# Four engines read the attention test's sum itself, TensorE alone reads the copy, and the copy sits in the fourth-last row's buffer

## The chip, the cores and the metric

The kernel runs on one core of a Trainium2 chip: TensorE (PE), VectorE (DVE), ScalarE (ACT), GpSimd (POOL) and SyncE (SP), with 16 DMA engines. The metric is the device time of one execution in microseconds; lower is better.

## The reference

A window attention with four sink keys feeds a gated MLP block. Cut to what is computed:

```python
scores = q @ k.T / sqrt(64)                    # 4 batches, 8 heads, 768 x 768
keep   = (col < 4) | (0 <= row - col < 128)    # 4 sink keys and a window of 128
a      = softmax(where(keep, scores, -1e9))
x      = heads_side_by_side(a @ v)             # (4, 768, 512)
h      = gelu_tanh(x @ w_in)                   # (4, 768, 1024)
u, v   = halves(h)
v_n    = (v - mean(v)) / sqrt(var(v) + 1e-6) * g_ln
v_s    = w_sg @ v_n + b_sg                     # over the 768 positions
out    = x + (u * v_s) @ w_out                 # float32
```

## The kernel before, in words

**Two programs in one.** The main program takes the exponentials without subtracting the row maximum. That is good as long as every row sum and its reciprocal stay in range. A second, general program (`general`, from L1250) subtracts the maximum; it stands behind `tc.If(found["total"] < COUNT)` at L1306 and is skipped when the test says that the main program was good. The test is small: on GpSimd two comparisons of all reciprocals with bounds (`compare`), a product with ones on TensorE (`tally`), a sum on VectorE (`summed`), which leaves one integer, `total`. All of it is done in the last fifth of the kernel, ahead of the last batch's output rows.

**The branch.** Every engine has its own instruction stream and decides for itself, so each of the five has to load the integer into a register (`ask`, L1126, a TENSOR_LOAD in the trace) and then branches (L1306). SP loads `total` in the op `peek` and ACT in `peek_act`, both in the middle of the last batch. PE, DVE and POOL load it in the last op, `look`. They don't load `total` but a copy of it. The op `copied` (L1140) writes the copy on VectorE into column 0 of an output row's buffer, `held_o`. That buffer is the one of output row block `MARK`, and since it is being stored to HBM, the copy waits for that store to have landed. In this way the three engines reach the branch only when the copy is made.

**After the branch.** An engine that skips the general program adds to its own semaphore what the general program would have added. POOL does so too for the eight semaphores of its own DMA queue (waits on them, then one INC_SWDGE_SEM). Behind that come the instructions that end the program, which the trace puts at L1338: SP waits for the semaphores of all queues and engines, two in one wait, and then all engines meet in two rounds, with a clearing of the semaphores by POOL between them.

**Order.** Nothing is scheduled at run time: `FIRST` lists the names of all ops in the order in which they are emitted, and each engine runs its own in that order. `Planner.run` walks that list; a `Buf` is counted open in its room until its last user was emitted. The list ends in the last batch's output rows: `pj3t` (product on PE), `o3t` (residual added on DVE, L918) and `store3t` (SP, L928) for t = 2, 1, 0, 3, 4, 5, then row block 3 of batch 2, kept for last and cut in halves: `pj23x o23x store23x` with its store on SP, and `pj23y o23y store23y` with its store on ACT. Behind these stand `copied` and `look`. So block (3, 4), the `MARK` of the kernel before, is the third-last row block and block (3, 3) the fourth-last.

Of the kernel before, what the change touches and what calls it, by code (L numbers as in the profile page):

```python
# [9 lines left out]
I32 = mybir.dt.int32  # L10
# [39 lines left out]
class Planner:  # L50
# [15 lines left out]
    def add(self, *args, **kwargs):  # L66
        op = Op(*args, **kwargs)
        self.ops.append(op)
        return op
# [86 lines left out]
    "look"  # L156
)
TAKERS = (
    "zero_a0:ACT zero_a1:DVE zero_a2:DVE zero_a3:DVE low_a:DVE zero_b0:DVE zero_b1:DVE "
# [19 lines left out]
def kernel(  # L179
# [16 lines left out]
    B, H, S, Dh = q.shape  # L196
# [45 lines left out]
    add = plan.add  # L242
# [10 lines left out]
    WARM = 8  # L253
    AHEAD = (0, 1)
    LAST = (2, 3)
    MARK = (B - 1, 4)
    LONG = ()
    BY_DMA = (11,12,13,14,15)
    W_DMA = ()
# [21 lines left out]
    total = consts.tile([128, 1], I32, name="total")  # L281
# [53 lines left out]
    def make_mask(m, at):  # L335
        for h in range(2):
# [6 lines left out]
                    rank=-2000)  # L343
    T["dark0"] = add("dark0", {"DVE": 450}, lambda _: make_dark0(), [T["dark"]], use=[dark],
                     rank=-1998)
# [5 lines left out]
    if LONG:  # L351
        T["spread"] = add("spread", {"POOL": 900}, lambda _: make_spread(), new=[spread],
                          rank=-378)
# [658 lines left out]
    def turn_g(_):  # L1012
# [4 lines left out]
    a = add("turn_g", {"PE": 330}, turn_g, [T["g_row"], T["one"]], new=[g_ps], use=[g_row],  # L1017
            rank=9000)
# [39 lines left out]
    for n in range(NP):  # L1058
        r = 100 * n
# [26 lines left out]
    COUNT = 2 * 128 * NP * NT * 2  # L1086
    flat = rcps.rearrange("p n c i h o -> p (n c i h o)")

    def compare(_):
# [8 lines left out]
    a = add("compare", {"POOL": 900}, compare,  # L1098
            [T["rcp", n, c] for n in range(NP) for c in range(2)],
            new=[fits], rank=12000)  # L1100
# [8 lines left out]
    a = add("tally", {"PE": 180}, tally, [a], new=[ps], use=[fits], rank=12900)  # L1109
# [6 lines left out]
    a = add("summed", {"DVE": 500}, summed, [a], use=[ps], rank=12900)  # L1116
    found = {}
# [2 lines left out]
              mybir.EngineType.SP]  # L1120

    WHY = "a sum of so many zeros and ones"
    ASKED = [mybir.EngineType.SP, mybir.EngineType.Activation]

    def ask(tile, engines):
        return nc.values_load(tile[0:1, 0:1], engines=engines, min_val=0, max_val=COUNT,  # L1126
                              skip_runtime_bounds_check_because=WHY)

    def peek(_):
        found["SP"] = ask(total, ASKED[0:1])

    def peek_act(_):
        found["ACT"] = ask(total, ASKED[1:2])

    held_o = T["o_sb", *MARK]

# [2 lines left out]

    def look(_):
        tc.mark_branch_hint_location("rest", HINT, engines=HINTED)
        rest = ask(held_o.tile[:, 0:1].bitcast(I32), [e for e in mybir.ALL_ENGINES if e not in ASKED])
        found["total"] = type(rest).of_register_unchecked(
            type(rest.val)([*found["SP"].val, *found["ACT"].val, *rest.val]), min_val=0,
            max_val=COUNT)

    for part in segments:
        for lead, follow in zip(part[0::2], part[1::2]):  # L1150
# [2 lines left out]
            follow.rank = plan.first.get(follow.name, -10000)  # L1153
    for t in range(NT):
        T["pj", B - 1, t].behind.append(a)
    add("peek", {"SP": 750}, peek, [a], rank=0)
    add("peek_act", {"ACT": 750}, peek_act, [a], rank=0)
    T["st", -1, 0] = add("copied", {"DVE": 150}, copied, [a, T["st", *MARK]], use=[held_o],
                         rank=0)
    add("look", {"SP": 1200}, look, [a, T["st", -1, 0]] + [T["st", B - 1, t] for t in range(NT)], rank=0)  # L1160
    plan.run()

# [180 lines left out]
```

## Time and profile before

| | |
|---|---|
| Runs | 162.61, 162.88 and 165.15 us; median 162.88 us |
| The profiled execution | 162.92 us, of which the span of the trace is 160.9 us |
| Busy share of the span | PE 94%, DVE 82%, ACT 67%, POOL 52% |
| Granted TensorE clock | 0.998 |
| Instructions | 4016 |

The span goes from the first to the last instruction of the trace; some 2.0 us of the execution lie around it. A busy share is an average over the whole kernel; the change touches what happens behind the last output rows, so the stretch that counts is the last few microseconds.

### The profile page before, as it was taken

Reading aid. Unit: us, or ns where it says so; the run is one execution under the profiler, and the core shown is the slowest. Engines: PE = TensorE matmul, PEld = TensorE weight load, DVE = VectorE, ACT = ScalarE, POOL = GpSimd, SP = SyncE. Lnnn points to the kernel's source line nnn. Section 1 sums busy time; section 2 is a strip of 40 time slices with the busy share of each in tenths; the row PEclk is TensorE's granted clock in tenths of the full one; section 3 lists DMA queues with packets and bytes.
Section 4 is the critical chain, followed back from the end, with each engine's and each line's share of the span. In section 5 each row is a group of like instructions: output and inputs, shape, how many; then the busy total and the mean of one; then the engine's idle time right before and its main releaser. Section 6 shows DMA issues by size and latency. Waiting matters only on the chain.

```text
span 160.9 us, 4016 instructions
## 1 busy us (share of the span) xinstructions
PE 151.2 (94%) x1562; PEld 87.7 (55%) x1562; DVE 132.3 (82%) x283; ACT 107.6 (67%) x143; POOL 83.5 (52%) x126
## 2 busy tenths in 40 slices
PE   6899999999999999999799999998999999999960
PEld 2454574667657576456555664545556545555530
DVE  7556887798897999789999989589999969888960
ACT  6198787897979797979686875747995187701100
POOL 3645944155899695287957743573779403200000
PEclk9999999999999999999999999999999999999999
DMA  4999999998999956999876879799966330130182
GB/s 152 332 247 311 194 169 201 203 304 265 344 306 295 275 143 182 328 238 259 141 218 154 194 188 257 131 297 256 215 172 175 114 130 0 65 134 0 65 322 82
DMA packets 67877, 32.42 MB, mean 201 GB/s; under 512 B 56564, under 2 KB 64772, under 8 KB 67856
## 3 DMA queue, kind: packets, MB, share of 16 engines
q1 hardware_dynamic: 65328, 29.26, 70.1%
q0 software_dynamic: 2384, 2.75, 10.6%
q8 instruction: 13, 0.21, 0.6%
q10 hardware_dynamic: 144, 0.13, 0.2%
q14 instruction: 8, 0.07, 0.1%
HBM read 24.81 MB, written 6.29 MB: 193 GB/s over the span
## 4 chain that ended last, share of the span: by engine, by line
PE 79%; DVE 8%; POOL 4%; DMA 4%; ACT 1%; issue 1%; SPq 0%; DVEq 0%; POOLq 0%; ACTq 0%
PE vs L864 20%; PE hv L751 11%; PE o_ps L907 11%; PE hu L793 10%; PE sc L610 9%; PE av L676 8%; PE cps L550 4%; PE sc L590 3%; DMA q_f<-in_q_dram 2%; DVE vn L840 2%; PE xps L726 2%; POOL mv L820 2%; DVE o_sb L918 2%; DMA out_dram<-o_sb 2%; DVE mv L826 1%; DVE ex L638 1%
## 5 line engine op out<-in xcount | busy, mean ns | idle before, releaser
L627 ACT ACTIVATE ex<-sc 128x1024 bf16<-128x1024 f32 x48 | 47.4, 1024 | 9.7 <-PE sc L610 9.6
L864 PE MATMUL vs<-wsgT,vn 128*128 128x384 bf16 x192 | 35.5, 326 | 1.4 <-DVE vn L840 1.1
L864 PEld LDWEIGHTS <-vn 128*128 128x128 bf16 x192 | 17.5, 98 | 13.1 <-DVE vn L840 1.5
L793 PE MATMUL hu<-xT,w_in_sb 128*128 128x384 bf16 x128 | 23.6, 326 | 0.8 <-DVE o_sb L918 0.8
L801 ACT ACTIVATE uT<-hu 128x384 bf16<-128x384 f32 x32 | 14.9, 489 | 12.3 <-PE hu L793 12.1
L907 PE MATMUL o_ps<-w_out_sb,gT 128*128 128x512 bf16 (+1 forms) x100 | 23.1, 371 | 0.0
L751 PE MATMUL hv<-w_in_sb,xT 128*128 128x512 bf16 x96 | 22.5, 379 | 0.0
L875 DVE SCALAR_TENSOR_TENSOR vs<-vs,g_sb,b_bc 128x384 f32<-128x384 f32 x32 | 19.6, 621 | 2.8 <-PE vs L864 1.2
L773 DVE BATCH_NORM_STATS2 st<-v_all 128x6 f32<-128x512 f32 x24 | 16.3, 677 | 6.3 <-ACT v_all L762 6.3
L249 POOL CAST cast<-k_f 128x768 bf16<-128x768 f32 x16 | 13.7, 858 | 14.1 <-DMA k_f<-in_k_dram 12.8
L610 PE MATMUL sc<-qT,kT 64*128 64x256 bf16 (+2 forms) x320 | 18.9, 249 | 0.4 <-ACT qT L247 0.4
L311 POOL TENSOR_SCALAR_AFFINE_SELECT ex<-ex 128x512 bf16<-128x512 bf16 (+1 forms) x23 | 15.1, 655 | 7.9 <-ACT ex L627 7.7
L676 PEld LDWEIGHTS <-ex 128*128 128x128 bf16 x480 | 16.7, 97 | 4.1 <-issue 1.4
L695 DVE TENSOR_TENSOR x<-av,rcps 128x384 bf16<-128x384 f32 x32 | 17.5, 552 | 0.9
L883 DVE TENSOR_TENSOR gT<-vs,uT 128x384 bf16<-128x384 f32 x32 | 17.5, 556 | 0.9
L676 PE MATMUL av<-v_sb,ex 128*128 128x65 bf16 x352 | 18.0, 194 | 0.1
L249 POOL CAST cast<-q_f 128x768 bf16<-128x768 f32 x15 | 13.1, 872 | 9.7 <-issue 4.6
L793 PEld LDWEIGHTS <-w_in_sb 128*128 128x128 bf16 x128 | 12.3, 98 | 9.7 <-issue 1.2
L918 DVE TENSOR_TENSOR o_sb<-o_ps,x 128x512 f32<-128x512 f32 (+1 forms) x25 | 16.2, 663 | 1.3 <-PE o_ps L907 1.2
L762 ACT ACTIVATE v_all<-hv 128x512 f32<-128x512 f32 x24 | 13.7, 598 | 5.2 <-PE hv L751 5.0
L249 POOL CAST v_sb<-v_f 128x768 bf16<-128x768 f32 x16 | 13.9, 869 | 2.3 <-DMA v_f<-in_v_dram 2.3
L751 PEld LDWEIGHTS <-xT 128*128 128x128 bf16 x96 | 9.2, 98 | 10.5 <-DVE xT L249 0.6
(71 smaller groups left out, 197.6 us busy)
## 6 DMA issues: line engine op xcount, KB each, us to landing
k_f<-in_k_dram SPq DMA_DIRECT2D x16, 384.0 KB, 5.9
q_f<-in_q_dram SPq DMA_DIRECT2D x16, 384.0 KB, 5.1
v_f<-in_v_dram SPq DMA_DIRECT2D x16, 384.0 KB, 5.9
out_dram<-o_sb SPq DMA_DIRECT2D x23, 256.0 KB, 2.2
wsg<-in_moe_w_sg_dram POOLq DMA_DIRECT2D x2, 576.0 KB, 10.5
w_in_sb<-in_moe_w_in_dram POOLq DMA_DIRECT2D x2, 512.0 KB, 7.6
w_out_sb<-in_moe_w_out_dram POOLq DMA_DIRECT2D x1, 512.0 KB, 7.8
b_bc<-in_moe_b_sg_dram SPq DMA_DIRECT2D x1, 384.0 KB
```

Of the source, the lines that this page charges most:

```text
L249: eng[e].tensor_copy(dst, src)
L610: nc.tensor.matmul(sc.tile[row:row + keys, h, col:col + m], kT.tile[rows, k0:k0 + keys], qT.tile[rows, q0:q0 + m], start=not by_pe, stop=n ...
L627: nc.scalar.activation(out=ex.tile, in_=sc.tile, func=AF.Exp, scale=scale)
L676: nc.tensor.matmul(av.tile[:, m, h, :], ex.tile[:, h, col:col + 128], val, start=first, stop=(m == HT - 1 and h == 1 and at == len(steps) ...
L695: nc.vector.tensor_mul(x.tile[:, hp, HT * c:HT * (c + 1), :].rearrange("p i (h d) -> p i h d", h=2), av.tile[:, :, :, 0:64], rcp.to_broadc ...
L751: nc.tensor.matmul(ps.tile[:, 0:512], xT.tile[:, c, 128 * j:128 * (j + 1)], w_in_sb[:, c, DF:], start=(c == 0), stop=(c == KD - 1))
L793: nc.tensor.matmul(ps.tile[:, 0:NH], w_in_sb[:, c, 128 * f:128 * (f + 1)], xT.tile[:, c, NH * m:NH * (m + 1)], start=(c == 0), stop=(c == ...
L864: nc.tensor.matmul(ps.tile[:, 0:NH], vn.tile[:, si, 128 * f:128 * (f + 1)], wsgT[:, si, cols], start=(si == 0), stop=(si == NT - 1))
L875: nc.vector.scalar_tensor_tensor(out=ps.tile[:, 0:NH], in0=ps.tile[:, 0:NH], scalar=g_sb[:, f:f + 1], in1=b_bc[:, cols], op0=ALU.mult, op1 ...
L883: nc.vector.tensor_mul(gT.tile[:, f, cols], ps.tile[:, 0:NH], uT.tile[:, f, cols])
L907: nc.tensor.matmul(ps.tile[:, 0:w], gT.tile[:, c, 128 * t:128 * (t + 1)], w_out_sb[:, c, cols], start=(c == 0), stop=(c == KU - 1))
L918: nc.vector.tensor_add(o_sb.tile[:, 0:w].rearrange("p (h d) -> p h d", d=128), ps.tile[:, 0:w].rearrange("p (h d) -> p h d", d=128), x.til ...
```

## The change

Three things are different. First, `MARK` goes from block (3, 4) to block (3, 3): the copy is written into the buffer of the row block stored one earlier. Second, POOL and DVE no longer load the copy in `look`; they load `total` itself, in ops of their own. `peek_POOL` stands directly behind `peek_ACT` in the list, where POOL has no op left behind it; `peek_DVE` stands behind `store23y`, that is behind DVE's last addition and ahead of `copied`. Third, `look` loads the copy for PE alone. The number of loads stays at five and no arithmetic changes.

```diff
-    "gT301 hu331 gelu_u331 peek_act store32 gT331 pj31 o31 store31 pj30 o30 store30 pj33 o33 "
-    "store33 pj34 o34 store34 pj35 o35 store35 pj23x o23x store23x pj23y o23y store23y copied "
-    "look"
+    "gT301 hu331 gelu_u331 peek_ACT peek_POOL store32 gT331 pj31 o31 store31 pj30 o30 store30 "
+    "pj33 o33 store33 pj34 o34 store34 pj35 o35 store35 pj23x o23x store23x pj23y o23y store23y "
+    "peek_DVE copied look"
...
-    MARK = (B - 1, 4)
+    MARK = (B - 1, 3)
...
-    ASKED = [mybir.EngineType.SP, mybir.EngineType.Activation]
+    EARLY = dict(SP=mybir.EngineType.SP, ACT=mybir.EngineType.Activation,
+                 POOL=mybir.EngineType.Pool, DVE=mybir.EngineType.DVE)
...
-    def peek(_):
-        found["SP"] = ask(total, ASKED[0:1])
-
-    def peek_act(_):
-        found["ACT"] = ask(total, ASKED[1:2])
+    def peek(e):
+        found[e] = ask(total, [EARLY[e]])
...
-        rest = ask(held_o.tile[:, 0:1].bitcast(I32), [e for e in mybir.ALL_ENGINES if e not in ASKED])
-        found["total"] = type(rest).of_register_unchecked(
-            type(rest.val)([*found["SP"].val, *found["ACT"].val, *rest.val]), min_val=0,
-            max_val=COUNT)
+        rest = ask(held_o.tile[:, 0:1].bitcast(I32),
+                   [e for e in mybir.ALL_ENGINES if e not in EARLY.values()])
+        regs = [r for e in EARLY for r in found[e].val] + list(rest.val)
+        found["total"] = type(rest).of_register_unchecked(type(rest.val)(regs), min_val=0,
+                                                          max_val=COUNT)
...
-    add("peek", {"SP": 750}, peek, [a], rank=0)
-    add("peek_act", {"ACT": 750}, peek_act, [a], rank=0)
+    for e in EARLY:
+        add("peek" if e == "SP" else f"peek_{e}", {e: 100 if e == "DVE" else 750}, peek, [a], rank=0)
```

## The prediction

> **What bounds the kernel now.** I read the page first, then the chain of work that ended last, then the last microseconds by stretches and by line.
>
> ```profile
> span 160.9 us, 4016 instructions
> PE 151.2 (94%) x1562; PEld 87.7 (55%) x1562; DVE 132.3 (82%) x283; ACT 107.6 (67%) x143; POOL 83.5 (52%) x126
> ```
>
> TensorE sets the time of nearly the whole kernel. The change touches no product, so what matters is what lies behind the last product. The chain in order of time, its last part (start, us, what), and two stretches (length, busy us of PE, PEld, DVE, ACT, POOL, clock, DMA share, GB/s):
>
> ```profile
> 150.33 3.47 PE o_ps L907 x16
> ...
> 153.82 0.70 DVE o_sb L918
> ...
> 154.54 2.72 DMA out_dram<-o_sb
> ...
> 157.35 0.15 DVE o_sb L1140
> ```
> ```profile
> 155.40:157.60 2.20, 0.12 (x2) 0.00 (x0) 0.79 (x3) 0.00 (x0) 0.00 (x0) 1.00 0.93 344
> 157.60:160.90 3.30, 0.00 (x0) 0.00 (x0) 0.00 (x0) 0.00 (x0) 0.00 (x0) 0.92 0.07 19
> ```
>
> PE ends at about 155.5. From there to 160.9 the core stores rows and ends the program. The chain doesn't run through the last store but through that of block (3, 4), issued at 154.54 and landed at 157.26: the copy at L1140 waits for it and ends at 157.50. The register loads (L1126), the branch (L1306) and the end of the program (L1338) follow (engine queue, operation, count, ns min/median/max, first and last start):
>
> ```profile
> L1126 SPq TENSOR_LOAD <-total x1: 517/517/517, 141.3 to 141.3; - x1
> L1126 ACTq TENSOR_LOAD <-total x1: 713/713/713, 150.4 to 150.4; - x1
> L1126 POOLq TENSOR_LOAD <-o_sb x1: 487/487/487, 157.5 to 157.5; - x1
> L1126 DVEq TENSOR_LOAD <-o_sb x1: 542/542/542, 157.5 to 157.5; - x1
> L1126 PEldq TENSOR_LOAD <-o_sb x1: 487/487/487, 157.5 to 157.5; - x1
> ```
> ```profile
> L1306 POOLq EVENT_SEMAPHORE  x5: 17/43/43, 158.6 to 158.9; - x5
> L1306 SPq COMPARE_BRANCH  x1: 67/67/67, 156.3 to 156.3; - x1
> L1306 ACTq COMPARE_BRANCH  x1: 68/68/68, 156.5 to 156.5; - x1
> L1306 ACTq EVENT_SEMAPHORE  x1: 17/17/17, 157.0 to 157.0; - x1
> L1306 POOLq COMPARE_BRANCH  x1: 45/45/45, 158.1 to 158.1; - x1
> L1306 PEldq COMPARE_BRANCH  x1: 393/393/393, 158.1 to 158.1; - x1
> L1306 DVEq COMPARE_BRANCH  x1: 90/90/90, 158.2 to 158.2; - x1
> L1306 PEldq EVENT_SEMAPHORE  x1: 51/51/51, 158.6 to 158.6; - x1
> L1306 DVEq EVENT_SEMAPHORE  x1: 21/21/21, 158.8 to 158.8; - x1
> L1306 POOLq INC_SWDGE_SEM  x1: 292/292/292, 159.0 to 159.0; - x1
> ```
> ```profile
> L1338 SPq EVENT_SEMAPHORE  x12: 28/28/28, 159.3 to 160.0; - x12
> L1338 SPq DRAIN  x2: 7/10/13, 160.0 to 160.1; - x2
> ...
> L1338 PEldq DRAIN  x2: 8/8/8, 158.7 to 160.4; - x2
> L1338 DVEq DRAIN  x2: 10/14/17, 158.9 to 160.4; - x2
> ```
>
> All three late readers load at 157.5 and branch at 158.1 to 158.2. PE and DVE are then through at 158.7 and 158.9. POOL has more to do: five waits from 158.6 and the INC_SWDGE_SEM from 159.0 to 159.3. SP, which had branched at 156.3, starts its row of twelve waits exactly then, at 159.3. Its own waits (engine, line, for what: us in total, times, longest) say how long it stood:
>
> ```profile
> SPq L1338 <- DMA w_out_sb<-in_moe_w_out_dram: 2.9, 1, 2.9
> ```
>
> The view names the load of w_out, which had landed some 100 us earlier. What SP really waits for is the count that POOL adds to this semaphore once it has skipped the general program. So the tail is: store of (3, 4), copy, POOL's load, POOL's branch, POOL's counts, then SP's twelve waits at 0.06 us each (0.7 us over 12) and 0.9 us of meeting, 160.0 to 160.9. The last stores landed meanwhile and cost nothing.
>
> **The change part by part.** *POOL's read* moves from 157.5 to where POOL has nothing left:
>
> ```profile
> 136.97 0.89 POOL L820 TENSOR_TENSOR mv<-mv,half 128x3 f32<-128x3 f32 x1
> ```
> ```profile
> 137.56 0.15 DVE L1114 CAST total<-count 128x1 int32<-128x1 f32 x1
> ```
>
> POOL ends its last work at 137.86 and the sum stands at 137.71. The load takes 0.49 us and the way from the branch to the end of INC_SWDGE_SEM 1.2 us (158.1 to 159.3), so POOL is through at about 139.6. SP asks for it only behind its branch at 156.3. The part costs nothing, with 17 us of cover; nothing stands behind the load on POOL but the branch. On the path it removes POOL's whole way.
>
> *The copy's buffer.* The copy now waits for the store of (3, 3). Issues of the stores (start, us) and their times to landing (queue, count, KB, median us):
>
> ```profile
> 154.68 1.35 DVE L918 TENSOR_TENSOR o_sb<-o_ps,x 128x512 f32<-128x512 f32 x3 [0.17 <-PE o_ps L907]
> ```
> ```profile
> 153.68 2.54 SPq L928 DMA_DIRECT2D out_dram<-o_sb  x4
> ```
> ```profile
> out_dram<-o_sb SPq DMA_DIRECT2D x6, 256.0 KB, 2.0
> out_dram<-o_sb SPq DMA_DIRECT2D x1, 128.0 KB, 2.4
> out_dram<-o_sb ACTq DMA_DIRECT2D x1, 128.0 KB, 2.5
> ```
>
> The first of SP's four issues, at 153.68, is block (3, 3): landed at 155.7 by the median of 2.0, at 156.4 with the 2.72 of its successor. DVE's last addition ends at 156.03, so this wait is gone or worth up to 0.4. The planner holds one buffer a little longer in a room of four, which adds no instruction.
>
> *DVE's read* now stands between the last addition and the copy, and the copy queues behind it, as does PE's read. No row shows a load directly behind a busy DVE. From below: ACT's load began at 150.4, when its last activation had just begun, so a load doesn't wait for the work ahead to end; then DVE's begins at about 155.65, takes 0.54 and ends at 156.2. From above: it begins only at 156.03 and takes ACT's 0.71, ending at 156.75. The store's 156.4 lies within this. With the copy's 0.15 and 0.1 of waits around it, the copy ends between 156.4 and 157.0; I take 156.5, by ACT's load, the nearest row. From the copy's end (157.5) PE needed 1.2 to its drain (158.7) and DVE 1.4 (158.9). So PE is through at 157.7 (bounds 157.6 and 158.2), and DVE, whose load no longer lies behind the copy, at the latest at 157.9 (bounds 157.8 and 158.4).
>
> *What is late next.* SP can now walk its twelve waits from about 156.8 (branch 156.3, and the 0.5 that ACT took from its branch to its next instruction). It stops where something isn't done, and the last thing is the store on ACT:
>
> ```profile
> 156.07 0.39 ACTq L928 DMA_DIRECT2D out_dram<-o_sb  x1
> ```
>
> It lands 2.5 after 156.07, at 158.57: behind PE and DVE even at their upper bounds. In the trace's records that semaphore is in the ninth of the twelve waits, so four remain, 0.24, to 158.81; then the meeting, 0.9, to 159.7. (First in the row would give 160.2, last 159.5.) DVE's read and PE's copy are thus hidden by that landing; without this cover each 0.1 us of theirs behind it would cost 0.1.
>
> **The sum.** 160.9 less 159.7 is 1.2 us. The profiled execution took 162.92, which lies 0.04 above the median; less 1.2 this is 161.7, and the median less 1.2 rounds to the same.
>
> **The rivals.**
>
> *The last store lands sooner.* The two half stores took 2.4 and 2.5 us though they carry half of what the others carry in 2.0. With 2.0 the last one lands at 158.1, the span ends at 159.2, and the time is 161.2. Against it: they are issued when the DMA engines are 0.93 busy, which the change leaves as it is.
>
> *DVE's read is slow, and PE's copy is the last.* The load would have to take over 1.4 us instead of 0.5 to 0.7 before PE overtakes the landing. At 2 us behind 156.03 the copy ends at 158.3, PE at 159.5, and with two waits and the meeting left (0.1 and 0.9) the span is 160.5, the gain 0.4: 162.5. The five loads of the trace all speak against it.
>
> *The change doesn't do what it says.* If POOL's early counts don't free SP, because SP stands for another reason that the view hides, SP starts at 159.3 as before: 162.9. For it speaks only that the view names a DMA; against it that SP's first wait begins within the INC_SWDGE_SEM's 292 ns.
>
> *Instruction pages in front of the last store.* This is the one that can end slower. PE and DVE take their branch about 1.0 us earlier, at 157.1 or before, while the DMA engines still carry the last stores. Instruction pages go over the same engines (packets, MB, share of 16 engines' span):
>
> ```profile
> q8 instruction: 13, 0.21, 0.6%
> q14 instruction: 8, 0.07, 0.1%
> ```
>
> That is 0.006 x 16 x 160.9 / 13 = 1.2 us for a page of queue 8 and 0.3 for one of queue 14. A page that gets ahead of the ACT store's last packets on one DMA engine delays the landing by 0.3 to 1.2, and the time comes to 162.0 to 162.9; both on one engine, 1.5, and it is 163.2. It decides from a landing 1.2 later, at 159.8. Against it: 16 engines share these packets, and a page has to meet the last ones. "Branching breaks sequential prefetch", says the Trainium skill (Runtime: NRT & Kernel Launch, Instruction fetch mechanics): a taken branch to a page not at hand waits for a DMA to fetch it, and by that rule a jump into loaded DMA engines is the dearer one. The trace shows the gap behind each branch but no such dependence: ACT's from 156.5 to 157.0 at 0.93 busy is no longer than POOL's, 158.1 to 158.6, at 0.07.
>
> **How the numbers follow.** The forecast, 161.7, gets 0.66. The store that lands sooner (161.2) 0.08, the slow read (162.5) 0.08, no effect (162.9) 0.08, the pages 0.10, half of it under 162.9 and half above. The range from 160.9 to 163.0 holds all but the dear end of the pages and the scatter of runs (162.61 to 162.92 among those near each other). A difference of 2%, 3.3 us, is about what a measurement of this kernel can tell from no change. No case gets there: the whole tail behind the last product is 5.4 us, of which a landing and the meeting remain in any case, and the dearest stall is 1.5 over the forecast. Faster by over 2% gets 0.02, within 2% 0.94, slower 0.04, for what the rows don't show.
>
> **What would show it.** POOL's load near 137.9 and its INC_SWDGE_SEM by 140; SP's idle time at its waits ending near 158.6, with the last store landing and not POOL's counts as its end; only the last few of SP's twelve waits behind that; the copy ending near 156.5 instead of 157.5; PE's drain near 157.7; a span of 159.7. Wrong would be: SP's long wait still ending in POOL or in PE, a TENSOR_LOAD over 1 us on DVE, the last store landing later than 2.5 us after its issue, or a change of PE's end near 155.5.

## The result and the profile after

The changed kernel took 161.94 us in the median of 20 runs, the kernel before 162.69 us in 20 runs beside them. The ratio is 0.9939, with a 95% interval from 0.9914 to 0.9963: about 1.0 us faster (0.6 to 1.4), well inside 2%. In a second series, 12 runs of the change beside 30 of the kernel before, it came to 0.9929 (0.9894 to 0.9965). The profile below is from that second series, labelled e11_after, since the first profiled execution of the change was a slow one, as was that of e3 below. In the profiles the last product ends at different times (154.7 to 156.7 us, without e10 and e12), so the times of each profile are read against its own last product.

```profile
span 159.3 us, 4016 instructions
...
PE 151.0 (95%) x1562; PEld 87.8 (55%) x1562; DVE 130.9 (82%) x283; ACT 107.5 (67%) x143; POOL 83.6 (52%) x126
```

The end of the work in the timeline (start, us, engine, line):

```profile
151.79 3.19 PE L907 MATMUL o_ps<-w_out_sb,gT 128*128 128x512 bf16 x18
...
154.15 1.35 DVE L918 TENSOR_TENSOR o_sb<-o_ps,x 128x512 f32<-128x512 f32 x3 [0.17 <-PE o_ps L907]
155.53 0.38 ACTq L928 DMA_DIRECT2D out_dram<-o_sb  x1
155.73 0.15 DVE L1138 COPY o_sb<-total 128x1 int32<-128x1 int32 x1 [0.23 <-DVE o_sb L918]
```

The last product ends at 154.98; from there to the end of the span are 4.3 us. In the kernel before it was 5.4 (155.5 to 160.9). The copy now stands 0.2 us behind DVE's last addition, not 1.3 us behind it waiting for a store. The register loads and the branches of the change:

```profile
L1127 POOLq TENSOR_LOAD <-total x1: 486/486/486, 137.2 to 137.2; - x1
L1127 SPq TENSOR_LOAD <-total x1: 516/516/516, 140.8 to 140.8; - x1
L1127 ACTq TENSOR_LOAD <-total x1: 722/722/722, 149.8 to 149.8; - x1
L1127 DVEq TENSOR_LOAD <-total x1: 543/543/543, 155.0 to 155.0; - x1
L1127 PEldq TENSOR_LOAD <-o_sb x1: 768/768/768, 155.9 to 155.9; - x1
```
```profile
L1305 POOLq COMPARE_BRANCH  x1: 45/45/45, 137.8 to 137.8; - x1
L1305 POOLq INC_SWDGE_SEM  x1: 292/292/292, 138.7 to 138.7; - x1
L1305 SPq COMPARE_BRANCH  x1: 68/68/68, 155.7 to 155.7; - x1
L1305 DVEq COMPARE_BRANCH  x1: 84/84/84, 155.8 to 155.8; - x1
...
L1305 DVEq EVENT_SEMAPHORE  x1: 21/21/21, 156.8 to 156.8; - x1
L1305 PEldq COMPARE_BRANCH  x1: 393/393/393, 156.8 to 156.8; - x1
L1305 PEldq EVENT_SEMAPHORE  x1: 51/51/51, 157.3 to 157.3; - x1
```

POOL reads and branches more than 20 us before the end; its counts are added by 139.0. What SP waits for at the end (engine, line, for what: us in total, times, longest), and its twelve waits:

```profile
SPq L1337 <- DMA out_dram<-o_sb: 1.4, 2, 0.8
...
SPq L1337 <- PEq L1127: 0.4, 1, 0.4
```
```profile
L1337 SPq EVENT_SEMAPHORE  x12: 27/28/28, 155.9 to 158.4; - x12
```
```profile
out_dram<-o_sb SPq DMA_DIRECT2D x1, 128.0 KB, 2.3
out_dram<-o_sb ACTq DMA_DIRECT2D x1, 128.0 KB, 2.6
```

The 2.9 us under the name of w_out's load are gone. SP starts its waits at 155.9 and is now held by stores (one wait, 0.4 us, is put down to PE's load of the copy). The last store, issued at 155.53, lands 2.6 later, at 158.2; the last waits and the meeting end the span at 159.3, 1.1 later.

### The profile page after: what moved, and what is told of

Same layout as the page of the kernel before. It is cut to its first block, busy times and chain, and to the rows that moved or that the text cites. A ratio compares the mean times of both kernels' runs of the same rounds, so it can differ in the third digit from the quotient of the medians.

```text
span 161.1 us, 4001 instructions
## 1 busy us (share of the span) xinstructions
PE 150.1 (93%) x1547; PEld 87.3 (54%) x1562; DVE 130.5 (81%) x283; ACT 107.5 (67%) x143; POOL 83.6 (52%) x126
## 5 line engine op out<-in xcount | busy, mean ns | idle before, releaser
L907 PE MATMUL o_ps<-w_out_sb,gT 128*128 128x512 bf16 (+1 forms) x91 | 22.6, 370 | 0.5
```

The lines of the kernel that those rows point to most:

```text
L907: nc.tensor.matmul(ps.tile[:, 0:w], gT.tile[:, c, 128 * t:128 * (t + 1)], w_out_sb[:, c, cols], start=(c == 0), stop=(c == KU - 1))
```

## The experiments

The theory of the two ends: the program ends with the later of two chains, POOL's counts followed by SP's twelve waits, or the last store's landing (or PE or DVE, where they are later) followed by the waits behind it. The first ended the kernel before, the second ends the change. Rivals: the three parts add up; the copy's place alone is the term; instruction pages in front of the last stores take part of the gain back. All ratios are to the kernel before, run beside. The last column is read from one profile each, from the end of the last product to the end of the span. The intervals of e1, e4, e5 and e9 overlap with that of the change, so what tells these kernels apart is less the time than what SP waits for in the profiles.

| kernel | ratio (95% interval) | last product to end, us |
|---|---|---|
| before | | 5.4 |
| the change | 0.9929 (0.9894 to 0.9965) | 4.3 |
| e1, POOL's read alone | 0.9944 (0.9919 to 0.9970) | 4.5 |
| e2, the copy's place alone | 1.0100 (1.0067 to 1.0133) | 7.1 |
| e3, DVE's read alone | 0.9978 (0.9944 to 1.0011) | 5.4 |
| e4, all but POOL's read | 0.9963 (0.9929 to 0.9998) | 4.6 |
| e5, copy in the second-last row's buffer | 0.9962 (0.9934 to 0.9990) | 4.9 |
| e6, no branch hints | 1.0063 (1.0025 to 1.0100) | 6.7 |
| e7, last store left out | 0.9885 (0.9828 to 0.9942) | 3.9 |
| e8, no copy, PE reads the sum | 0.9998 (0.9960 to 1.0036) | 5.8 |
| e9, e2 with a hint for POOL | 0.9942 (0.9910 to 0.9973) | 4.7 |
| e10, sixteen memsets near the start | 1.0071 (1.0032 to 1.0109) | 4.2 |
| e12, ten memsets near 129 us | 1.0060 (1.0019 to 1.0101) | 4.2 |

**The parts one by one.** e1, POOL's read alone:

```diff
-    MARK = (B - 1, 3)
+    MARK = (B - 1, 4)
-    "peek_DVE copied look"
+    "copied look"
-    EARLY = dict(SP=..., ACT=..., POOL=..., DVE=...)
+    EARLY = dict(SP=..., ACT=..., POOL=...)
```

> Only POOL reads the sum itself; the copy stays in the third-last row's buffer, and DVE and PE read it. Theory of the two ends: the program ends either with POOL's counts and twelve waits of SP behind them, or with the last store's landing and four waits; POOL's read alone takes the first away. Then SP's long wait ends in the store's landing, or 0.2 us later in DVE's and PE's way behind the copy at 157.5, and this part alone brings 0.9 to 1.1 us (ratio about 0.994). Rival, the parts add up: the copy's place and DVE's read bring their own shares, and this part alone brings about a third, 0.3 us. Rival, the copy's wait is the term: no gain.

It brought 0.0056 of 162.45, 0.9 us, nearly the whole gain. What SP waited for in e1:

```profile
SPq L1336 <- DVEq L1126: 1.5, 1, 1.5
...
SPq L1336 <- DVEq L1304: 0.3, 1, 0.3
SPq L1336 <- DMA out_dram<-o_sb: 0.2, 1, 0.2
```

POOL is gone from the list. SP's last real wait is on DVE (L1304, 0.3 us), which in this kernel still reads behind the late copy: the 0.2 us that the expectation gave for it. So the parts don't add up as thirds.

e2, the copy's place alone (the change without `peek_POOL` and `peek_DVE`):

```diff
-    "gT301 hu331 gelu_u331 peek_ACT peek_POOL store32 ..."
+    "gT301 hu331 gelu_u331 peek_ACT store32 ..."
-    "peek_DVE copied look"
+    "copied look"
-    EARLY = dict(SP=..., ACT=..., POOL=..., DVE=...)
+    EARLY = dict(SP=..., ACT=...)
```

> Only the copy's buffer changes, to the fourth-last row's; POOL, DVE and PE all read the copy as before. Two ends: the copy comes at 156.3 instead of 157.5, POOL's counts end 1.75 us behind it, at 158.1, still ahead of the last landing at 158.6; so this part alone also brings the whole gain, 1.0 to 1.2 us (ratio about 0.993), and the parts don't add up. Rival, the parts add up: about a third, 0.3 us. Rival, POOL's early read is needed: no gain, SP's long wait still ends in POOL's counts.

It was 1.6 us slower, which no theory had said. The copy did come early, 0.4 us behind the last product. POOL's rows of this kernel at the branch show what happened next, with what SP waited for:

```profile
L1304 POOLq EVENT_SEMAPHORE  x5: 17/43/43, 161.5 to 161.8; - x5
...
L1304 POOLq COMPARE_BRANCH  x1: 45/45/45, 158.1 to 158.1; - x1
...
L1304 POOLq INC_SWDGE_SEM  x1: 300/300/300, 161.9 to 161.9; - x1
```
```profile
SPq L1336 <- DMA w_out_sb<-in_moe_w_out_dram: 4.6, 1, 4.6
```

POOL branches at 158.1 and does its next instruction at 161.5, 3.3 us behind the branch's end. In the profiles of the change and of the kernel before this gap is 0.4 us. While POOL stood, three pages of instructions were fetched on queue 14 (158.2 to 161.4 us; queue: packets, MB, share):

```profile
q14 instruction: 3, 0.02, 2.7%
```

The view doesn't say which of the three, if any, is POOL's. POOL is the one engine without a branch hint in this kernel, so e9 gave it one (all else as in e2):

```diff
     HINTED = [mybir.EngineType.PE, mybir.EngineType.Activation, mybir.EngineType.DVE,
-              mybir.EngineType.SP]
+              mybir.EngineType.SP, mybir.EngineType.Pool]
```

> Only the copy's buffer changes, as in the run that came out 1.6 us slower, and POOL gets a branch hint as the four other engines have. In that run POOL's next instruction came 3.3 us behind its branch, against 0.4 in every other run. If POOL's branch waited there for its instruction page, the hint brings the 3.3 us to about 0.5, POOL's counts end about 1.75 us behind the copy, ahead of the last landing, and the run is 0.7 to 1.1 us faster than the kernel before, as the theory of the two ends had said of this part. Rival, POOL waits for something else (its data or a semaphore): the gap stays near 3.3 us and the run is 1.6 us slower than the kernel before.

```profile
L1304 POOLq EVENT_SEMAPHORE  x5: 17/42/43, 157.1 to 157.4; - x5
...
L1304 POOLq COMPARE_BRANCH  x1: 65/65/65, 156.6 to 156.6; - x1
```
```profile
SPq L1336 <- DMA out_dram<-o_sb: 0.4, 1, 0.4
```

The gap is 0.5 us and the run 0.9 us faster than the kernel before. SP stops once more behind its wait for POOL's counts, for a store, so POOL is off the end by 0.4 us. So POOL had waited in e2 for the code that it jumps to, and without that wait the copy's place alone brings the gain too. (The hint is also one instruction more in POOL's stream, which shifts the code behind it. Whether the hint or the shift cured the wait was not tried apart; both act on the code, not on POOL's data or semaphores.) Either of the two parts takes POOL's chain out of the end. Why the code was at hand in the kernel before, in e3 and in e4, which have the same POOL instructions and no hint either, and not in e2, stays open.

e3 (DVE's read alone, `MARK` as before) and e4 (all but POOL's read); in both, POOL also leaves `EARLY`:

```diff
 e3 -    MARK = (B - 1, 3)                       e4 -    ... peek_ACT peek_POOL store32 ...
    +    MARK = (B - 1, 4)                          +    ... peek_ACT store32 ...
    -    ... peek_ACT peek_POOL store32 ...
    +    ... peek_ACT store32 ...
```

> Only DVE reads the sum itself, behind its last addition; the copy stays in the third-last row's buffer, and POOL and PE read it. Two ends: the copy still waits for its store until about 157.3, POOL's counts still end at 159.3 and hold SP: no gain, within 0.1 us (ratio 0.999 to 1.001). Rival, the parts add up: 0.3 us faster. A DVE load that holds the copy would show as a copy later than 157.4.

> The change without POOL's early read: the copy in the fourth-last row's buffer, DVE reads the sum itself, POOL and PE read the copy. Two ends: the copy ends between 156.5 and 157.3 by DVE's load, POOL's counts 1.75 us later, 158.3 to 159.1, about with the last landing (158.6 to 159.0 on the same scale): 0.8 to 1.2 us faster, as the whole change or up to 0.3 less. Rival, the parts add up: two thirds, 0.7 us. Rival, POOL's read is the term: no gain.

SP's long wait in e3 and then in e4:

```profile
SPq L1336 <- DMA w_out_sb<-in_moe_w_out_dram: 2.9, 1, 2.9
```
```profile
SPq L1336 <- DMA w_out_sb<-in_moe_w_out_dram: 2.1, 1, 2.1
```

e3 keeps the 2.9 of the kernel before and its 5.4 us behind the last product; the ratio's interval holds 1, so a small gain isn't excluded. In e4 POOL's chain is still what ends SP's wait, but 0.8 us sooner, and the run is 0.6 us faster (0.03 to 1.2). That is less than the 0.8 to 1.2 expected and as near to the 0.7 of the rival that adds the parts up; what speaks against that rival is e1, not e4.

**The end of the change.** e5 puts the copy behind a later store, e7 leaves the last store out, so that its last half row is missing from the result:

```diff
 e5 -    MARK = (B - 1, 3)                       e7 -    queue = nc.scalar if i else nc.sync
    +    MARK = (B - 1, 5)                          +    if i:
                                                    +        return
                                                    +    queue = nc.sync
```

> The change with the copy in the second-last row's buffer instead of the fourth-last's. The copy then waits for a store issued 1.7 us later. Two ends, with PE's way as a third: the copy ends at about 158.1 on the scale of the kernel before, PE is through 1.2 later, at 159.3, behind the last landing at 158.6; with two waits and the meeting the gain over the kernel before shrinks from 1.0 to about 0.5 us (ratio 0.997), and SP's last long wait ends in PE. Rival, PE's copy has slack whatever its place, because PE branches into code at hand: ratio as the change, 0.994.

> The change without the last store, the half row that ACT sends; that half row is left out of the result. Two ends: the last landing is now that of SP's half row store, 0.2 to 0.6 us earlier, and with less queued; the tail shortens by 0.3 to 0.8 us until PE's way (drain 1.2 us behind the copy) takes over. Rival, the landing isn't what ends the kernel: no change against the change itself.

PE's rows at the branch of e5 and what SP waited for:

```profile
L1305 PEldq COMPARE_BRANCH  x1: 388/388/388, 158.1 to 158.1; - x1
L1305 PEldq EVENT_SEMAPHORE  x1: 51/51/51, 158.6 to 158.6; - x1
```
```profile
SPq L1337 <- PEq L1127: 1.9, 1, 1.9
...
SPq L1337 <- PEq L1305: 0.4, 1, 0.4
```

With the later copy PE is the last, and the tail is 0.5 us longer than the change's. In e7 SP's waits at the end, ahead of the meeting, are for the remaining stores alone, and the tail is 0.4 shorter:

```profile
SPq L1339 <- DMA out_dram<-o_sb: 1.4, 3, 0.6
```

Both ways the end follows the landing or PE, whichever is later.

**Instruction pages.** e8 lets PE read the sum itself behind its last product and drops the copy; e6 takes the hints away:

```diff
 e8 -    "peek_DVE copied look"                  e6 -    HINTED = [PE, Activation, DVE, SP]
    +    "peek_DVE peek_PE look"                    +    HINTED = []
    -    T["st", -1, 0] = add("copied", ...)
```

> All five engines read the sum itself, PE behind its last product; the copy is gone. Two ends: PE was not the last in the change, so nothing is gained on this account: as the change within 0.1 us (ratio to the kernel before 0.994). Rival, instruction pages in front of the last store: PE branches at about 156 instead of 157.5 to 158.3 and fetches its page of 16 KiB, 1.2 us on one DMA engine, while the stores are still in flight: the last landing is up to 1.2 us later and the gain over the kernel before is gone or turns into a loss of 0.2 us.

> The change without the branch hints on four engines. The profile of the change shows the last packet of each of the last three stores landing 0.4 to 1.0 us behind the other fifteen engines' packets. If the instruction pages that the hints fetch cause this, one page near 156.7 on the trace is gone, the last store lands in 2.0 to 2.2 us instead of 2.5 to 3.0, and the run is 0.4 to 0.8 us faster than the change, unless PE's and DVE's branches now wait for their pages behind it and take that back. If the late packets have another cause, the landing stays at 2.5 to 3.0 and the run is as the change or slower by what the branches cost, up to 1 us on PE.

e8: PE's branch, then pages and stores of the stretch 154 to 157 us (queue: packets, MB, share; then KB and us to landing):

```profile
L1301 PEldq COMPARE_BRANCH  x1: 393/393/393, 153.6 to 153.6; - x1
```
```profile
q8 instruction: 1, 0.02, 3.6%
q14 instruction: 2, 0.02, 1.7%
...
out_dram<-o_sb SPq DMA_DIRECT2D x1, 128.0 KB, 4.4
out_dram<-o_sb ACTq DMA_DIRECT2D x1, 128.0 KB, 3.8
```

One 16 KiB page for PE (3.6% of 16 engines over 3 us, 1.7 us on one of them) stands among the stores, which land in 4.4 and 3.8 us instead of 2.3 and 2.6. SP's issue of its half row, begun at 155.0, took 2.05 us itself; in the change the longest of these three took 0.38 (count, ns min/median/max):

```profile
L928 SPq DMA_DIRECT2D out_dram<-o_sb x3: 332/333/2052, 153.7 to 155.0; - x3
```

So the half row on SP left late as a whole, not by one packet. The gain is gone: the rival with the pages is real, and in the change the copy keeps it away by holding PE back. PE also branched before its last product had ended (153.6 against 154.7), not behind it as expected; its stream runs ahead of its products.

e6, at the branches:

```profile
L1304 ACTq COMPARE_BRANCH  x1: 54/54/54, 156.4 to 156.4; - x1
L1304 PEldq COMPARE_BRANCH  x1: 3698/3698/3698, 157.3 to 157.3; - x1
L1304 ACTq EVENT_SEMAPHORE  x1: 17/17/17, 159.2 to 159.2; - x1
L1304 DVEq EVENT_SEMAPHORE  x1: 21/21/21, 160.1 to 160.1; - x1
```

PE's branch takes 3.7 us instead of 0.4, so PE loses 3.3, not the 1 us at most that had been expected. ACT's next instruction comes 2.7 us behind its branch instead of 0.4, and DVE's 3.8 instead of 0.9. SP lost its hint too and goes on 0.1 us behind its branch as before. Here and in e2 the trace agrees with what the prediction cited from the Trainium skill (Runtime: NRT & Kernel Launch, Instruction fetch mechanics), that a taken branch to a page not at hand waits for its fetch, and gives it a price, 2.7 to 3.8 us. Not every branch without a hint pays it: SP's here and POOL's in most kernels did not. The page near the last product's end was still fetched, at 155.5, and the last store still took 2.8, so the hints don't cause it.

e10 and e12 move that page by adding instructions to DVE's stream:

```diff
 e10 -   cols_k0 cast_k1 turn_q0                 e12 -   gT201 hv30
     +   cols_k0 pad cast_k1 turn_q0                 +   gT201 pad hv30
 both +  spare = consts.tile([128, 1], F32, name="spare")
      +  def pad():
      +      for _ in range(16):                     # e12: 10
      +          nc.vector.memset(spare, 0.0)
```

> The change with sixteen small memsets more on DVE near the start, in its idle time behind the first copy of k. In every run one page of instructions (queue 14) is fetched within 0.5 us of the last product's end, and the last three or four stores each land one packet 0.4 to 1.2 us late. If the page is DVE's, read when its stream crosses a page's edge, sixteen more instructions ahead move it some 6 us earlier, before the last stores; their landings shrink to 2.0 to 2.1 us and the run is 0.3 to 0.6 us faster than the change. If the page belongs to another engine, it stays where it is and the run is as the change. If the late packets have another cause, the page moves and the landings stay at 2.4 to 3.0.

> The change with ten small memsets on DVE in its 1.4 us of idle time ahead of the last batch's statistics (near 129 us), instead of sixteen at the start, where they cost 0.5 us on the first batch and a stretch of halved TensorE clock. The page moves from 154.8 to about 150 to 151, ahead of the last four stores; the three stores on SP land in 2.0 to 2.1 us, ACT's half row in 2.0 to 2.5, since pages behind the branches of DVE and PE still meet it. The end comes 0.1 to 0.5 us earlier than the change's (4.0 to 4.3 us from the last product to the end, against 4.34), ratio to the kernel before 0.989 to 0.993. If the memsets don't fit into the idle time, up to 0.5 us of this is lost and the run is as the change.

The pages, first of the change between 154 and 156.5 us, then of e12 between 151 and 153, and the two half rows' stores of e12:

```profile
q14 instruction: 1, 0.01, 1.3%
```
```profile
q14 instruction: 1, 0.01, 1.1%
```
```profile
out_dram<-o_sb SPq DMA_DIRECT2D x1, 128.0 KB, 2.0
out_dram<-o_sb ACTq DMA_DIRECT2D x1, 128.0 KB, 2.5
```

The page moved, in e12 to 5.7 us before the last product's end (152.0 to 157.7), and SP's half row lands in 2.0 us as the whole rows do, not 2.3: as far as these two runs go, the page is DVE's and made the late packets. The tail is 4.2 us, 0.1 less than the change's, since ACT's half row still takes 2.5. But both kernels are slower as a whole, where both had been expected faster than the change. In e12 it isn't the memsets: it loses time all along, long before them; TensorE is busy for 45.3 of its first 50 us, in the change for 47.2. The loads of e12 and then of the change (KB, median us to landing):

```profile
k_f<-in_k_dram SPq DMA_DIRECT2D x16, 384.0 KB, 6.8
...
v_f<-in_v_dram SPq DMA_DIRECT2D x16, 384.0 KB, 7.2
```
```profile
k_f<-in_k_dram SPq DMA_DIRECT2D x16, 384.0 KB, 5.9
...
v_f<-in_v_dram SPq DMA_DIRECT2D x16, 384.0 KB, 5.8
```

What e10 and e12 have besides the memsets is one more constant of one element per partition, declared behind the other constants. Whether it moves the buffers behind it and so slows the loads was not tried apart. No complete version was shown to beat the change.

e11, the change again, whose numbers stand in the table:

> The change itself again, beside the others of this call: 0.6% faster than the kernel before (ratio 0.991 to 0.997), the last store landing 2.4 to 3.0 us behind its issue, and SP's long waits ending in the stores' landings.

## Why the prediction was right, point by point

- **What held the end.** Right, and shown by e1: with POOL's read alone SP's wait under w_out's name is gone and 0.9 of the 1.0 us is there.
- **POOL's part costs nothing.** Right: read at 137.2, counts done by 139.0, SP's first wait at 155.9.
- **DVE's read and the copy.** Predicted between two bounds, with the lower one (a load beside the last addition) nearer: it began at 155.0, ahead of the last addition's end at 155.5, and took 0.54; the copy ended 0.38 behind that addition (155.88 against 155.50), where 0.37 to 0.97 had been given and 0.47 taken. The copy's idle time is put down to that addition, not to the store of (3, 3): that wait is gone.
- **PE's way.** Mis-sized: from the copy's end to its drain 1.6 us instead of 1.2. PE's load took 0.77 and not 0.49. In the profiles PE's load took 0.75 to 0.80 where it began up to 0.6 us behind the last store's issue, and 0.49 where it began 1.5 us or more behind it. PE was through 0.7 us ahead of the last landing (157.5 against 158.2), where 0.9 had been predicted; in e5 it came 0.8 behind it (158.7 against 157.9).
- **SP's start.** Mis-sized without effect: 0.2 us behind its branch, not 0.5.
- **The last landing ends the kernel.** Right, by SP's waits and by e7. The landing took 2.6 where 2.5 had been taken, which the prediction had listed as a sign of being wrong; behind it came 1.1 us, as predicted.
- **The sum.** 1.2 predicted, 1.0 measured (0.6 to 1.4); the tail in the two profiles went from 5.4 to 4.3. What the tail lacks of the 1.2 is the landing, 3.2 us behind the last product where 3.05 had been taken. The remaining 0.5 of the spans' difference (160.9 and 159.3) lies ahead of the last product, where executions differ.
- **The rivals.** The pages were the right thing to fear, at 0.10, but for a reason that the prediction didn't have: not PE's and DVE's branches in the change itself, but PE's without the copy (e8) and an engine whose code isn't at hand (e2). In the change the copy holds PE's branch back, and DVE, which branches early, is through at 156.9, well ahead of the last landing. The prediction also saw no sign that the gap behind a branch depends on what the DMA engines carry; DVE's went from 0.5 to 0.9 us in the change (more on this at the end). The rival of a sooner landing (161.2) did not come, but what was held against it, the loaded DMA engines, wasn't the reason: in e12, with the engines about as busy (0.85 against 0.89 in the 3.2 us around the last product's end), SP's half row landed in 2.0 once the page was out of its way. The prediction saw two things that take POOL off the end as parts of one sum; they are alternatives, and one of them alone is a loss without a hint.

## What to carry to other kernels

Where a wait at the end carries the name of something that ended long ago, look for who else counts on that semaphore; here it was an engine that came to its branch 1.8 us after SP. Before moving a branch or a read earlier, ask what code it will fetch and past which transfers: the same part was worth 0.9 us with the code at hand and cost 1.6 us without. And compare tails from the last product's end, since executions differ by more ahead of it than the change was worth.

## What the runs showed of the hardware that was not expected

- Counted from the branch's end, the next instruction came 0.1 to 0.5 us behind a taken branch with a hint. DVE's came 0.9 to 1.2 us behind where it branched within 1.0 us of the start of the page near the last product's end (the change, e4, e7, e8), and 0.5 in the other runs with its hint, in e10 and e12 too, where stores ran but that page had moved. Without a hint, ACT took 2.7 and DVE 3.8, PE 3.7 for the branch itself (e6), but SP 0.1 (e6) and POOL 0.4 or 3.3, by kernel.
- One 8 KiB page of instructions makes the last packet of each store late that is in flight or issued behind it: half a row lands in 2.3 instead of 2.0. With a 16 KiB page there too it was 4.4, and the issue of a store took 2.05 us instead of 0.38.
- A register load took 0.47 to 0.61 us or 0.71 to 0.81. PE's was a long one close behind the last store's issue, but DVE's, 0.5 us ahead of that issue, was a short one (0.54); what decides stays open.
- PE's stream ran ahead of its products: in e8 it branched 1.1 us before its last product had ended.
